# Softmax weights transposed two heads at a time, and value products on quarters of the array

## The chip, the cores and the metric

The kernel runs on one core of one Trainium2 chip. The metric is the device time of one execution in microseconds (us). The engines named here are TensorE (PE: matmuls and transposes, with its weight loads listed apart as PEld), VectorE (DVE), ScalarE (ACT), GpSimd (POOL) and SyncE (SP, which issues every DMA of this kernel).

## The reference

Three stages follow one another: attention over short windows, a gated feed-forward layer and a feed-forward layer with a rational activation. The change lies in the first one.

```python
# attention: q, k, v are [4, 8, 768, 64]; chunks of 32 queries; 8 memory keys per head
for c in range(24):
    keys   = concat(mem_k, k[16 before the chunk : 8 behind it])   # 8 + 16 + 32 + 8 = 64 keys
    scores = q_c @ keys.T / 8
    a = exp(scores - max(scores));  a = a / (sum(a) + 1e-9)
    out[chunk] = a @ values                                        # the same 64 positions of v
x = out, heads side by side                                        # [3072, 512]
x = ((1 / (1 + exp(-(x @ w_gate)))) * (x @ w_val)) @ w_out         # 512 -> 1536 -> 512
h = x @ w_in                                                       # 512 -> 2048
g = (a0 + a1*h + a2*h^2 + a3*h^3) / (1 + |b0|*|h| + |b1|*h^2 + 1e-6)
return g @ w_out2                                                  # 2048 -> 512
```

## The kernel before

**Tiles.** The 3072 tokens are 24 attention tiles `t` of 128 queries: four chunks of 32, all eight heads. Neighbouring chunks go in pairs: a window `g` holds the 104 positions that its two chunks reach together (`WIN` = 104, of which each chunk uses 64, `KEYS`; the second chunk's 64 begin at `OFF1` = 40). The head number is `2r + h`.

**Attention of one tile**, by the names in the code:

- `attn_qk` (line 104): 32 matmuls into two PSUM tiles `sp`, one for each `h`. Each multiplies 32 queries by 64 keys over 64 numbers of a head, so it uses 64 rows and 32 columns of the array. Scores lie with queries on partitions and the 64 keys along the row.
- `attn_max`, `attn_exp`, `attn_sum`: the softmax on VectorE and ScalarE, in the tile `s` (128 x 8 heads x 64 keys).
- `attn_mul` (line 157): two VectorE multiplications, one for each chunk of a pair (64 partitions each), write the weights into a buffer `a` with 104 positions per head. Each chunk's weights go to its own place in the window, and the rest of `a` is zero (set once by GpSimd, lines 67 and 68).
- `attn_t` (lines 170 and 172): eight transposes on TensorE, one per head (128 queries x 104 positions), into two PSUM tiles `tp`, and two ScalarE copies to `at`.
- `attn_pv` (line 184): 16 matmuls into one PSUM tile `xp`, over the 104 positions of a window, 64 columns of the array each, 64 moving columns (the two chunks of the window). Line 192 (ScalarE) and line 193 (VectorE) write it out as a rounded high part and a low part, both in the tile `x`, which four tiles `t` fill together.

In the trace every plain fp32 matmul of lines 104 and 184 has two records, each with a weight load of its own: 64 records for the 32 matmuls of `sp`, 32 for the 16 of `xp`. Transposes have one.

**The feed-forward layers.** All their operands are split into a high and a low part, and three of the four cross products are summed, each a 128x512 matmul. The first layer runs over six blocks `j` of 512 tokens and twelve steps `f`; a step is two groups of 12 matmuls into `h` (line 261) and 12 into `acc` (line 293). The second layer (lines 342 and 381) follows the same way and has no attention in it.

**The order.** It is written out by hand. The attention of tiles 0 to 3 comes first, mixed with the unpacking of the first weights. Then the 72 steps of the first layer run, and a plan gives the attention of the tiles of the next block to certain steps: `attn_qk` and `attn_max` behind the second `h` group, `attn_sum`, `attn_mul`, `attn_pv` and `attn_t` between the two `h` groups. The PSUM tiles `sp`, `tp`, `xp` and `h` share four buffers that are handed out in turn (`psp`). Each engine works through its own list in order.

**The start.** SyncE issues its loads in one queue, in this order: q and k of tiles 0, 1 and 2, v of tiles 1 and 0, q and k of tile 3, three weight pieces of step 0, v of tile 3, the three of step 1, v of tile 2, the three of step 2. Of the v loads, the one for tile 2 is the last that tiles 0 to 3 need.

Of the kernel before, what the change touches and what calls it, by code (L numbers as in the profile page):

```python
# [8 lines left out]
F32 = mybir.dt.float32  # L9
# [4 lines left out]
ACTF = mybir.ActivationFunctionType  # L14
ALU = mybir.AluOpType
# [3 lines left out]
B, H, S, D = 4, 8, 768, 64  # L19
CH, LEFT, RIGHT, NMEM = 32, 16, 8, 8  # L20
NT, DM, DFF1, DFF2 = B * S, H * D, 1536, 2048
P = 128
NF1, NF2 = DFF1 // P, DFF2 // P
KT = DM // P
SB = S // P
NBLK = NT // P
CTX = LEFT + 2 * CH + RIGHT
WIN = NMEM + CTX + NMEM
KEYS = NMEM + LEFT + CH + RIGHT
OFF1 = WIN - KEYS  # L30
NSET = 8
KW, VW = NSET * WIN, 2 * DM
MASKED = -3.0e38
QC = 1.0 + 1e-6
BLOCKS1 = [512] * 6
# [4 lines left out]
def fused_kernel(ctx: ExitStack, tc: tile.TileContext, q, k, v, w1, w2, coef, x2d, w2d, out):  # L40
# [7 lines left out]
    nc = tc.nc  # L48

    const = ctx.enter_context(tc.tile_pool(name="const", bufs=1))  # L50
    wpool = ctx.enter_context(tc.tile_pool(name="w", bufs=32))
    xpool = ctx.enter_context(tc.tile_pool(name="x", bufs=2))
    gpool = ctx.enter_context(tc.tile_pool(name="g", bufs=4))
    tpool = ctx.enter_context(tc.tile_pool(name="t", bufs=11))
    spool = ctx.enter_context(tc.tile_pool(name="s", bufs=4))
    accp = ctx.enter_context(tc.tile_pool(name="acc", bufs=1, space=PSUM))
    psp = ctx.enter_context(tc.tile_pool(name="ps", bufs=4, space=PSUM))
# [1 line left out]
    ident = const.tile([P, P], F32, name="ident")  # L59
    make_identity(nc, ident)  # L60
    cf = const.tile([P, 6], F32, name="cf")
    cab = const.tile([P, 2], F32, name="cab")


    a_buf = [const.tile([P, NSET, WIN], F32, name=f"a{i}") for i in range(2)]
    for a in a_buf:
        nc.gpsimd.memset(a[0:64, :, KEYS:WIN], 0.0)
        nc.gpsimd.memset(a[64:128, :, 0:OFF1], 0.0)

    def t2(name):  # L70
        return tpool.tile([P, 512], F32, tag="t", name=name)

    def ps(name):
        return psp.tile([P, 512], F32, tag="ps", name=name)


    qs, ks, vs, s_sb, sc_ps, at_sb = {}, {}, {}, {}, {}, {}
# [5 lines left out]
        nc.sync.dma_start(out=u, in_=k[t])  # L83

    def load_v(t):
        u = vs[t] = wpool.tile([P, VW], F32, tag="w", name=f"v{t}")
        nc.sync.dma_start(out=u[0:WIN], in_=v[t])

    def edge(t):
        return t % SB in (0, SB - 1)  # L90

    def attn_qk(t):


        qt = qs.pop(t)
        kt = ks.pop(t).rearrange("p (r g w) -> p r g w", r=4, g=2)
        sps = [ps(f"sp{t}_{h}")[:, 0 : 4 * KEYS].rearrange("p (r w) -> p r w", r=4) for h in range(2)]
        for r in range(4):
            for i in range(4):
                c, g = divmod(i, 2)  # L100
                for h in range(2):
                    d = slice(64 * h, 64 * h + 64)
                    o = slice(32 * i, 32 * i + 32)
                    nc.tensor.matmul(  # L104
                        sps[h][o, r],
                        lhsT=qt[d, r, o],
                        rhs=kt[d, r, g, c * OFF1 : c * OFF1 + KEYS],
                        start=True,
                        stop=True,
                    )  # L110
        s = s_sb[t] = tpool.tile([P, NSET, KEYS], F32, tag="t", name=f"s{t}")
        sv = s.rearrange("p (r h) w -> p r h w", h=2)
        if edge(t):
            for h in range(2):
                nc.scalar.activation(out=sv[:, :, h], in_=sps[h], func=ACTF.Copy)
            if t % SB == 0:
                nc.gpsimd.memset(s[0:32, :, NMEM : NMEM + LEFT], MASKED)
            else:
                e = CTX - RIGHT + NMEM - OFF1
                nc.gpsimd.memset(s[96:128, :, e : e + RIGHT], MASKED)  # L120
        else:
            sc_ps[t] = sps
# [22 lines left out]
    rs = {}  # L145
# [6 lines left out]
        nc.vector.reciprocal(out=r, in_=r)  # L152

    def attn_mul(t):
        s, r, a = s_sb.pop(t), rs.pop(t), a_buf[t % 2]
        for lo, c0 in ((0, 0), (64, OFF1)):
            nc.vector.tensor_tensor(
                out=a[lo : lo + 64, :, c0 : c0 + KEYS],
                in0=s[lo : lo + 64],
                in1=r[lo : lo + 64].to_broadcast([64, NSET, KEYS]),  # L160
                op=ALU.mult,
            )

    def attn_t(t):
        a = a_buf[t % 2]
        at_sb[t] = []
        for half in range(2):
            tp = ps(f"tp{t}_{half}")
            for i in range(4):
                nc.tensor.transpose(tp[0:WIN, i * P : (i + 1) * P], a[:, 4 * half + i], ident)  # L170
            at = t2(f"at{t}_{half}")
            nc.scalar.activation(out=at[0:WIN], in_=tp[0:WIN], func=ACTF.Copy)
            at_sb[t].append(at)

    def attn_pv(t, x, n0):
        vt = vs.pop(t)[0:WIN].rearrange("p (g e) -> p g e", g=2)
        ats = at_sb.pop(t)
        xp = ps(f"xp{t}").rearrange("p (r n) -> p r n", r=4)
        for r in range(4):
            at = ats[r // 2][0:WIN].rearrange("p (s c g q) -> p s g c q", s=4, c=2, g=2)  # L180
            for g in range(2):
                for h in range(2):
                    e = (2 * r + h) * D
                    nc.tensor.matmul(  # L184
                        xp[64 * h : 64 * h + 64, r, 64 * g : 64 * g + 64],
                        lhsT=vt[:, g, e : e + D],
                        rhs=at[:, 2 * (r % 2) + h, g],
                        start=True,
                        stop=True,
                    )  # L190
        hi, lo = x[:, :, 0, n0 : n0 + P], x[:, :, 1, n0 : n0 + P]
        nc.scalar.activation(out=hi, in_=xp, func=ACTF.Copy)  # L192
        nc.vector.tensor_tensor(out=lo, in0=xp, in1=hi.bitcast(F32), op=ALU.subtract)

# [203 lines left out]
    def pv(t):  # L400
        j, n0 = t // 4, t % 4 * P
        if n0 == 0:
            xt[j] = xpool.tile([P, KT, 2, 512], F32R, tag="x", name=f"x{j}")
        attn_pv(t, xt[j], n0)
# [54 lines left out]
    for t in range(4, NBLK, 2):  # L459
        j, i = divmod(t, 4)  # L460
        s0 = (j - 1) * NF1 + (5 if i else 0)
        if j == 1:
            s0 = 5 if i else 2
        for o, u in ((0, t), (1, t + 1)):
            at(s0 + o - 2, load_qk, u)
            at(s0 + o, attn_qk, u)
            at(s0 + o, attn_max, u)
            at(s0 + 3, attn_exp, u)
            at(s0 + o + 3, load_v, u)
            at(s0 + o + 3, attn_sum, u)  # L470
            at(s0 + o + 3, attn_mul, u)
            at(s0 + o + 4, attn_t, u)
            at(s0 + o + 5, pv, u)
# [21 lines left out]
    with tc.manual_schedule():  # L495
# [3 lines left out]
        load_qk(1)  # L499
        load_qk(2)  # L500
        load_v(1)
        load_v(0)
        load_qk(3)
        load_w1(0)
# [3 lines left out]
        load_v(2)  # L508
        load_w1(2)
        attn_qk(0)  # L510
        attn_max(0)
        attn_exp(0)
        attn_qk(1)
        attn_qk(2)
        attn_sum(0)
# [5 lines left out]
        conv_scale("1_0_0")  # L521
        attn_exp(2)
        attn_mul(0)
        attn_mul(1)
        attn_max(3)
        attn_t(0)
        attn_sum(2)
        attn_exp(3)
        attn_sum(3)
        attn_t(1)  # L530
        conv_scale("1_0_2")
        attn_mul(2)
# [66 lines left out]
        for si in range(PRE, len(steps2) + LAG2):  # L599
            if si < len(steps2):  # L600
                j, f = steps2[si]
# [19 lines left out]
def _windows(k, mem):  # L621

    import numpy as np

    pad = np.zeros((B, H, LEFT + S + RIGHT, D), k.dtype)
    pad[:, :, LEFT : LEFT + S] = k
    n = S // (2 * CH)
    ctx = np.stack([pad[:, :, 2 * CH * g : 2 * CH * g + CTX] for g in range(n)], axis=2)
    m = np.broadcast_to(mem[:, :, None], (B, H, n, NMEM, D))
    return np.concatenate([m, ctx, m], axis=3)  # L630
# [52 lines left out]
```

## Time and profile before

| | before |
|---|---|
| time, median of 3 runs | 1221.54 us (1219.17 to 1221.76) |
| profiled execution | 1218.23 us, of which the span of the trace is 1216.5 us |
| TensorE busy | 1193.0 us, 98% of the span |
| VectorE busy | 906.7 us, 75% |
| ScalarE busy | 760.5 us, 63% |
| DMA traffic | 99.25 MB, mean 82 GB/s |

The share of busy time is a mean over the whole span; what matters for the change is the stretch in which attention runs, and which wait ends last there. Matmul records overlap (the next begins before the last one ends), so the cost of a small matmul is not its record's length but the distance to the next one: the length of a run of them, less one record, divided by the number less one.

### The profile page before, as it was taken

How to read it: one execution, taken by the hardware profiler on the slowest of the kernel's cores; microseconds unless marked ns; L12 is line 12 of the kernel's file. 1: busy time of each engine (PE TensorE's matmuls, PEld its weight loads, DVE VectorE, ACT ScalarE, POOL GpSimd, SP SyncE). 2: the span in 40 equal slices, each digit the busy share in tenths (PEclk: the TensorE clock that was granted, in tenths of full speed). 3: DMA queues.
4: the chain of work that ended last, by engine and by line, in shares of the span. 5: the costliest groups of instructions: out<-in, count | busy, mean ns of one | idle time of the engine just before them, and what ended most of it. 6: DMA issues, size and time to landing. Idle time of an engine off the chain costs nothing.

```text
span 1216.5 us, 18667 instructions
## 1 busy us (share of the span) xinstructions
PE 1193.0 (98%) x7392; PEld 981.5 (81%) x7392; DVE 906.7 (75%) x1458; ACT 760.5 (63%) x1302; POOL 3.5 (0%) x19
## 2 busy tenths in 40 slices
PE   4999999999999999999999999999999999999998
PEld 4787788888888888888888888888888888888887
DVE  6899566657566664765566589998898898898885
ACT  4987354545454554545555588777676776766765
POOL 0000000000000000000000000000000000000000
PEclk9899999999999999999999999999999999999999
DMA  9863041424243332512342110010100100100000
GB/s 309 313 197 123 23 143 53 134 88 136 66 146 108 107 103 75 169 54 80 126 152 87 33 63 18 10 53 9 44 18 9 53 18 1 52 18 1 35 1 35
DMA packets 39327, 99.25 MB, mean 82 GB/s; under 512 B 4488, under 2 KB 4488, under 8 KB 39240
## 3 DMA queue, kind: packets, MB, share of 16 engines
q1 hardware_dynamic: 39240, 98.06, 25.3%
q8 instruction: 58, 0.95, 0.3%
q14 instruction: 29, 0.24, 0.1%
HBM read 77.07 MB, written 20.97 MB: 81 GB/s over the span
## 4 chain that ended last, share of the span: by engine, by line
PE 89%; DVE 5%; ACT 3%; DMA 2%; issue 1%; SPq 0%; POOL 0%; DVEq 0%; POOLq 0%; ACTq 0%
PE h L261 28%; PE acc L381 21%; PE h L342 21%; PE acc L293 14%; PE xp L184 2%; PE tp L170 1%; DVE wf L218 1%; DVE wp L248 1%; DVE wf L225 1%; PE sp L104 1%; DMA v<-v_in 1%; DMA st<-w_in 1%; ACT g L279 1%; DVE sg L273 0%; ACT wp L244 0%
## 5 line engine op out<-in xcount | busy, mean ns | idle before, releaser
L261 PE MATMUL h<-x,wp 128*128 128x512 f32 x1728 | 414.8, 393 | 2.6 <-ACT x L192 1.6
L261 PEld LDWEIGHTS h<-x,wp 128*128 128x128 f32 x1728 | 323.8, 189 | 70.8 <-ACT x L192 1.8
L342 PE MATMUL h<-x,wp 128*128 128x512 f32 x1152 | 276.6, 389 | 0.0
L381 PE MATMUL acc<-wp,g 128*128 128x512 f32 x1152 | 276.0, 389 | 0.0
L381 PEld LDWEIGHTS acc<-wp,g 128*128 128x128 f32 x1152 | 216.3, 188 | 44.9
L342 PEld LDWEIGHTS h<-x,wp 128*128 128x128 f32 x1152 | 216.3, 188 | 44.8
L293 PE MATMUL acc<-g,wp 128*128 128x512 f32 x864 | 211.0, 393 | 0.0
L293 PEld LDWEIGHTS acc<-g,wp 128*128 128x128 f32 x864 | 160.7, 188 | 35.2
L279 ACT ACTIVATE g<-sg 128x512 fp32r<-128x512 f32 x72 | 45.5, 632 | 183.5 <-DVE sg L273 183.4
L350 ACT ACTIVATE t<-h,cf 128x512 f32<-128x512 f32 x96 | 74.7, 778 | 127.0 <-PE h L342 126.0
L273 DVE TENSOR_TENSOR sg<-sg,h 128x512 f32<-128x512 f32 x72 | 49.5, 687 | 123.8 <-PE h L261 106.4
L248 DVE TENSOR_TENSOR wp<-wf,wp 128x512 fp32r<-128x512 f32 x216 | 136.3, 685 | 0.1
L244 ACT ACTIVATE wp<-wf 128x512 fp32r<-128x512 f32 x216 | 120.8, 620 | 5.9 <-DVE c L225 4.0
L353 DVE TENSOR_TENSOR t<-t,h 128x512 f32<-128x512 f32 x96 | 65.9, 686 | 45.0 <-ACT hh L352 43.2
L270 ACT ACTIVATE sg<-h 128x512 f32<-128x512 f32 x72 | 42.9, 596 | 86.1 <-PE h L261 86.0
L280 DVE TENSOR_TENSOR g<-sg,g 128x512 fp32r<-128x512 f32 x72 | 49.9, 693 | 51.2 <-ACT g L279 51.2
L354 DVE SCALAR_TENSOR_TENSOR t<-t,cf,h 128x512 f32<-128x512 f32 x96 | 71.8, 748 | 3.4
L368 DVE SCALAR_TENSOR_TENSOR qq<-qq,y 128x512 f32<-128x512 f32 x96 | 65.9, 686 | 11.2 <-ACT y L363 11.2
L362 ACT ACTIVATE y<-qq,qc 128x512 f32<-128x512 f32 x96 | 70.0, 729 | 5.3 <-DVE qq L355 4.6
L355 DVE SCALAR_TENSOR_TENSOR qq<-hh,cab,qq 128x512 f32<-128x512 f32 x96 | 71.7, 747 | 0.0
L369 DVE SCALAR_TENSOR_TENSOR t<-t,cf,y 128x512 f32<-128x512 f32 x96 | 71.7, 747 | 0.0
L370 DVE SCALAR_TENSOR_TENSOR t<-qq,t 128x512 f32<-128x512 f32 x96 | 66.5, 693 | 3.3
(53 smaller groups left out, 930.8 us busy)
## 6 DMA issues: line engine op xcount, KB each, us to landing
st<-w_in SPq DMA_DIRECT2D x68, 512.0 KB, 7.1
k<-k_in SPq DMA_DIRECT2D x24, 416.0 KB, 6.9
v<-v_in SPq DMA_DIRECT2D x24, 416.0 KB
w2d<-c SPq DMA_DIRECT2D x32, 256.0 KB, 2.0
w2f<-w2d SPq DMA_DIRECT2D x32, 256.0 KB, 3.2
q<-q_in SPq DMA_DIRECT2D x24, 256.0 KB, 11.4
x2d<-x2s SPq DMA_DIRECT2D x24, 256.0 KB, 2.8
x2f<-x2d SPq DMA_DIRECT2D x24, 256.0 KB
```

What stands on the lines that cost most here:

```text
L244: nc.scalar.activation(out=wp[key][:, 0], in_=src, func=ACTF.Copy)
L248: nc.vector.tensor_tensor(out=t[:, 1], in0=src, in1=t[:, 0].bitcast(F32), op=ALU.subtract)
L261: nc.tensor.matmul(pt, lhsT=w[:, a, kt * P : (kt + 1) * P], rhs=x[:, kt, b, c0 : c0 + n], start=(kt == 0 and i == 0), stop=(kt == KT - 1 a ...
L293: nc.tensor.matmul(acc[j][d][:, c0 : c0 + n], lhsT=w[:, a, d * P : (d + 1) * P], rhs=g[:, b, 0:n], start=(f == 0 and c0 == 0 and i == 0), ...
L342: nc.tensor.matmul(hp, lhsT=w[:, a, kt * P : (kt + 1) * P], rhs=x[:, kt, b], start=(kt == 0 and i == 0), stop=(kt == KT - 1 and i == 2),)
L350: nc.scalar.activation(out=t, in_=hp, func=ACTF.Identity, scale=cf[:, 3:4], bias=cf[:, 2:3])
L354: nc.vector.scalar_tensor_tensor(out=t, in0=t, scalar=cf[:, 1:2], in1=hp, op0=ALU.add, op1=ALU.mult)
L355: nc.vector.scalar_tensor_tensor(out=qq, in0=hh, scalar=cab[:, 1:2], in1=qq, op0=ALU.mult, op1=ALU.add)
L362: nc.scalar.activation(out=y, in_=qq, func=ACTF.Abs_reciprocal_sqrt, bias=qc[:, 0:1])
L369: nc.vector.scalar_tensor_tensor(out=t, in0=t, scalar=cf[:, 0:1], in1=y, op0=ALU.add, op1=ALU.mult)
L370: nc.vector.scalar_tensor_tensor(out=t, in0=qq, scalar=2.0, in1=t, op0=ALU.subtract, op1=ALU.mult)
L381: nc.tensor.matmul(acc[j][m], lhsT=g[:, a, m * P : (m + 1) * P], rhs=w[:, b], start=(f == 0 and i == 0), stop=(f == NF2 - 1 and i == 2),)
```

## The change

The weights are no longer spread over a window of 104 positions. `attn_mul` multiplies in place, in one instruction over all 128 partitions, so that `s` holds 64 keys per head, and two heads lie side by side in 128 numbers. `attn_t` transposes such a pair at once: four transposes of 128x128 into one PSUM tile, and one copy. Behind it the 64 keys of head `h` = 0 lie on partitions 0 to 63 and those of `h` = 1 on partitions 64 to 127. `attn_pv` multiplies each chunk and each head by itself: 32 matmuls of 64 keys by 64 columns of the array by 32 queries, on one quarter of the array each (rows by `h`, columns by `e`, the low bit of the pair number), into two PSUM tiles, one for each `h`, that are written out in two halves. The values come laid out by chunk, 64 keys each on 128 partitions (512 KB per tile instead of 416 KB), and the rows of the first layer's weights are put into the new order of heads on the host. The GpSimd memsets of `a` go, and the pool `t` has 12 buffers instead of 11.

```diff
     def load_v(t):
-        u = vs[t] = wpool.tile([P, VW], F32, tag="w", name=f"v{t}")
-        nc.sync.dma_start(out=u[0:WIN], in_=v[t])
+        u = vs[t] = wpool.tile([P, 4, 4, D], F32, tag="w", name=f"v{t}")
+        nc.sync.dma_start(out=u, in_=v[t])
...
     def attn_mul(t):
-        s, r, a = s_sb.pop(t), rs.pop(t), a_buf[t % 2]
-        for lo, c0 in ((0, 0), (64, OFF1)):
-            nc.vector.tensor_tensor(
-                out=a[lo : lo + 64, :, c0 : c0 + KEYS],
-                in0=s[lo : lo + 64],
-                in1=r[lo : lo + 64].to_broadcast([64, NSET, KEYS]),
-                op=ALU.mult,
-            )
+        s, r = s_sb[t], rs.pop(t)
+        nc.vector.tensor_tensor(out=s, in0=s, in1=r.to_broadcast([P, NSET, KEYS]), op=ALU.mult)
 
     def attn_t(t):
-        a = a_buf[t % 2]
-        at_sb[t] = []
-        for half in range(2):
-            tp = ps(f"tp{t}_{half}")
+        s = s_sb.pop(t).rearrange("p (r h) w -> p r (h w)", h=2)
+        tp = ps(f"tp{t}")
+        for r in range(4):
+            nc.tensor.transpose(tp[:, r * P : (r + 1) * P], s[:, r], ident)
+        at = at_sb[t] = t2(f"at{t}")
+        nc.scalar.activation(out=at, in_=tp, func=ACTF.Copy)
...
+        vt, at = vs.pop(t), at_sb.pop(t).rearrange("p (r q) -> p r q", r=4)
+        xps = [ps(f"xp{t}_{h}")[:, 0:256].rearrange("p (k n) -> p k n", k=2) for h in range(2)]
+        for k in range(2):
             for i in range(4):
-                nc.tensor.transpose(tp[0:WIN, i * P : (i + 1) * P], a[:, 4 * half + i], ident)
-            at = t2(f"at{t}_{half}")
-            nc.scalar.activation(out=at[0:WIN], in_=tp[0:WIN], func=ACTF.Copy)
-            at_sb[t].append(at)
...
+                o = slice(32 * i, 32 * i + 32)
+                for e in range(2):
+                    for h in range(2):
+                        d = slice(64 * h, 64 * h + 64)
+                        nc.tensor.matmul(
+                            xps[h][64 * e : 64 * e + 64, k, o],
+                            lhsT=vt[d, i, 2 * k + e],
+                            rhs=at[d, 2 * k + e, o],
+                            start=True,
+                            stop=True,
+                        )
+        for h in range(2):
+            hi, lo = (x[:, 2 * h : 2 * h + 2, b, n0 : n0 + P] for b in range(2))
+            nc.scalar.activation(out=hi, in_=xps[h], func=ACTF.Copy)
+            nc.vector.tensor_tensor(out=lo, in0=xps[h], in1=hi.bitcast(F32), op=ALU.subtract)
```

The first place is TensorE in step 7 of block 0, between the two `h` groups, where the products of one tile and the transposes of the next stand (x8 means eight instructions alike). Before:

```order
L261 MATMUL h_7_0_0_1236<-x_368,wp_0_7_0_1090 128x512 x12
L184 MATMUL xp_1255<-at_0_1127,v_965 64x64 x8
L184 MATMUL xp_1255<-at_1_1134,v_965 64x64 x8
L170 MATMUL tp_0_1274<-ident,a_91 104x128 x4
L170 MATMUL tp_1_1281<-ident,a_91 104x128 x4
L261 MATMUL h_7_1_0_1288<-x_368,wp_0_7_1_1092 128x512 x12
```

The same place now, its beginning (the two `xp` rows alternate until there are 32 of them) and its end:

```order
L250 MATMUL h_7_0_0_1265<-x_344,wp_0_7_0_1127 128x512 x12
L172 MATMUL xp_0_1284<-at_1164,v_1003 64x32
L172 MATMUL xp_1_1285<-at_1164,v_1003 64x32
L172 MATMUL xp_0_1284<-at_1164,v_1003 64x32
L172 MATMUL xp_1_1285<-at_1164,v_1003 64x32
```

```order
L172 MATMUL xp_1_1285<-at_1164,v_1003 64x32
L157 MATMUL tp_1322<-ident,s_901 128x128 x4
L250 MATMUL h_7_1_0_1329<-x_344,wp_0_7_1_1129 128x512 x12
```

No instruction of another kind is moved past these: 16 products become 32 and eight transposes become four, at the same place in the step.

The second place is ScalarE in the start, from the copies of `xp` for tiles 1 and 2 to that for tile 3, with the unpacking of weights (`st`, `wp`) between them. Before:

```order
L192 ACTIVATE x_368<-xp_426 128x4x128
L192 ACTIVATE x_368<-xp_445 128x4x128
L213 ACTIVATE st_1_2_133<-st_1_2_133 128x512
L214 ACTIVATE st_1_2_133<-st_1_2_133 128x512
L244 ACTIVATE wp_0_0_1_466<-wf_366 128x512
L244 ACTIVATE wp_0_0_2_470<-wf_422 128x512
L192 ACTIVATE x_368<-xp_474 128x4x128
```

Now:

```order
L181 ACTIVATE x_344<-xp_0_445 128x2x128
L181 ACTIVATE x_344<-xp_1_446 128x2x128
L202 ACTIVATE st_1_2_127<-st_1_2_127 128x512
L203 ACTIVATE st_1_2_127<-st_1_2_127 128x512
L233 ACTIVATE wp_0_0_1_485<-wf_342 128x512
L233 ACTIVATE wp_0_0_2_489<-wf_403 128x512
L181 ACTIVATE x_344<-xp_0_493 128x2x128
L181 ACTIVATE x_344<-xp_1_494 128x2x128
```

Each copy has become two of half the size, and the four weight instructions between them stand where they stood.

## Rows read from the trace of the kernel before

**Rows 1.** Two stretches: length, busy us (instructions) of PE, PEld, DVE, ACT, POOL, clock, DMA share, GB/s.
```profile
0.00:34.08 34.08, 16.05 (x418) 13.52 (x418) 23.40 (x48) 18.65 (x35) 2.38 (x12) 0.92 0.97 320
34.08:590.00 555.92, 554.26 (x4229) 452.50 (x4230) 364.28 (x621) 314.87 (x546) 1.17 (x7) 1.00 0.37 116
```
**Rows 2.** Waits of TensorE: us in total, times, longest.
```profile
PE sp L104 <- DMA k<-k_in: 11.8, 4, 5.0
PE xp L184 <- DMA v<-v_in: 2.2, 1, 2.2
PE tp L170 <- DVE s L137: 1.0, 1, 1.0
```
**Rows 3.** Timeline of PE in block 1: start, length (both us), group, count.
```profile
183.71 1.03 PE L170 MATMUL tp<-ident,a 128*104 128x128 f32 x8
...
190.09 2.88 PE L261 MATMUL h<-x,wp 128*128 128x512 f32 x12
192.90 1.15 PE L184 MATMUL xp<-at,v 104*64 104x64 f32 x32
193.99 1.08 PE L170 MATMUL tp<-ident,a 128*104 128x128 f32 x8
...
197.76 0.86 PE L104 MATMUL sp<-k,q 64*32 64x64 f32 x64
```
**Rows 4.** Records of tp, xp, sp behind 40 us: ns min/median/max.
```profile
L170 PE MATMUL tp<-ident,a x160: 272/273/317, 88.3 to 574.6; 128*104 128x128 f32 x160
L184 PE MATMUL xp<-at,v x640: 221/222/270, 98.5 to 584.0; 104*64 104x64 f32 x160
L104 PE MATMUL sp<-k,q x1280: 212/216/243, 55.3 to 541.5; 64*32 64x64 f32 x183
L104 PEld LDWEIGHTS sp<-k,q x1280: 102/106/108, 55.3 to 541.4; 64*32 64x32 f32 x183
```
**Rows 5.** Timeline: sp begins; the first h behind xp; an h within a run.
```profile
92.02 0.12 PEld L104 LDWEIGHTS sp<-k,q 64*32 64x32 f32 x4 [0.35 <-ACT st L214]
...
110.94 0.50 PE L261 MATMUL h<-x,wp 128*128 128x512 f32 x1
...
211.94 0.39 PE L261 MATMUL h<-x,wp 128*128 128x512 f32 x1
```
**Rows 6.** Groups by line and form: busy us, mean ns | idle before.
```profile
L157 DVE TENSOR_TENSOR a<-s,r 64x512 f32<-64x512 f32 x48 | 32.8, 684 | 1.1
L172 ACT ACTIVATE at<-tp 104x512 f32<-104x512 f32 x48 | 26.0, 596 | 0.0
L193 DVE TENSOR_TENSOR x<-xp,x 128x512 fp32r<-128x512 f32 x24 | 16.6, 691 | 33.9 <-ACT x L192 33.9
L192 ACT ACTIVATE x<-xp 128x512 fp32r<-128x512 f32 x24 | 14.3, 595 | 10.5 <-PE xp L184 10.5
L137 DVE TENSOR_TENSOR s<-sp,m 128x256 f32<-128x256 f32 x32 | 12.0, 416 | 0.0
L115 ACT ACTIVATE s<-sp 128x256 f32<-128x256 f32 x16 | 5.1, 372 | 4.2 <-PE sp L104 4.2
```
**Rows 7.** Chain of waits in the start: start, length, what.
```profile
16.49 11.38 DMA v<-v_in
...
28.01 1.67 PE xp L184 x32
29.70 0.60 ACT x L192
```
**Rows 8.** Timeline of PE from 34 us.
```profile
34.08 5.15 PE L261 MATMUL h<-x,wp 128*128 128x512 f32 x12 [0.30 <-DVE x L193]
```
**Rows 9.** Two stretches of the start, columns as in Rows 1.
```profile
2.50:16.50 14.00, 4.69 (x256) 3.95 (x256) 8.36 (x20) 1.92 (x5) 0.59 (x3) 1.00 1.02 327
...
28.43:38.67 10.24, 8.32 (x69) 6.67 (x66) 8.33 (x15) 8.97 (x17) 0.00 (x0) 0.50 1.03 401
```
**Rows 10.** DMA issues: size and count of the v loads.
```profile
v<-v_in SPq DMA_DIRECT2D x24, 416.0 KB
```

More of the change, by code (lines that the diff above doesn't have):

```diff
@@ L31 @@
 NSET = 8
-KW, VW = NSET * WIN, 2 * DM
+KW = NSET * WIN
 MASKED = -3.0e38
@@ L53, in fused_kernel @@
     gpool = ctx.enter_context(tc.tile_pool(name="g", bufs=4))
-    tpool = ctx.enter_context(tc.tile_pool(name="t", bufs=11))
+    tpool = ctx.enter_context(tc.tile_pool(name="t", bufs=12))
     spool = ctx.enter_context(tc.tile_pool(name="s", bufs=4))
@@ L62, in fused_kernel @@
     cab = const.tile([P, 2], F32, name="cab")
[L65 to L68, printed above, removed]
     def t2(name):
@@ L99, in attn_qk @@
             for i in range(4):
-                c, g = divmod(i, 2)
+                g, c = divmod(i, 2)
                 for h in range(2):
@@ L175, in attn_pv @@
[L175 to L193, printed above, removed]
+        s, r = s_sb[t], rs.pop(t)
@@ new lines, in attn_mul, with attn_pv @@
+        nc.vector.tensor_tensor(out=s, in0=s, in1=r.to_broadcast([P, NSET, KEYS]), op=ALU.mult)
+    def attn_t(t):
+        s = s_sb.pop(t).rearrange("p (r h) w -> p r (h w)", h=2)
[4 more added lines that the diff above has]
+        nc.scalar.activation(out=at, in_=tp, func=ACTF.Copy)
+    def attn_pv(t, x, n0):
+        vt, at = vs.pop(t), at_sb.pop(t).rearrange("p (r q) -> p r q", r=4)
+        xps = [ps(f"xp{t}_{h}")[:, 0:256].rearrange("p (k n) -> p k n", k=2) for h in range(2)]
+        for k in range(2):
+            for i in range(4):
+                o = slice(32 * i, 32 * i + 32)
[13 more added lines that the diff above has]
+            nc.vector.tensor_tensor(out=lo, in0=xps[h], in1=hi.bitcast(F32), op=ALU.subtract)
@@ L639, with by_head @@
     a = {n: np.asarray(x) for n, x in inputs.items()}
-    qd = a["q"].reshape(B, 4, 2, SB, 2, 2, CH, D).transpose(0, 3, 2, 7, 1, 5, 4, 6)
+    qd = a["q"].reshape(B, 4, 2, SB, P, D).transpose(0, 3, 2, 5, 1, 4)
     kd = _windows(a["k"], a["mem_k"]).reshape(B, 4, 2, SB, 2, WIN, D)
     kd = kd.transpose(0, 3, 2, 6, 1, 4, 5)
-    vd = _windows(a["v"], a["mem_v"]).reshape(B, H, SB, 2, WIN, D)
-    vd = vd.transpose(0, 2, 4, 3, 1, 5)
+    vw = _windows(a["v"], a["mem_v"]).reshape(B, 4, 2, SB, 2, WIN, D)
+    vd = np.stack([vw[..., 0:KEYS, :], vw[..., OFF1:WIN, :]], axis=5)
+    vd = vd.transpose(0, 3, 2, 6, 4, 5, 1, 7)
+    heads = [2 * (2 * (kt % 2) + e) + kt // 2 for kt in range(KT) for e in range(2)]
     def cols(w, nf):
         return w.reshape(KT, P, nf, P).transpose(1, 2, 0, 3).reshape(P, nf, 512)
+    def by_head(w):
+        return w.reshape(H, D, -1)[heads].reshape(DM, -1)
     def rows(w, nf):
@@ L653 @@
     w1 = np.stack(
-        [cols(a["moe_w_gate"], NF1), cols(a["moe_w_val"], NF1), rows(a["moe_w_out"], NF1)], axis=2
+        [cols(by_head(a["moe_w_gate"]), NF1), cols(by_head(a["moe_w_val"]), NF1), rows(a["moe_w_out"], NF1)],
+        axis=2,
     )
@@ L660 @@
         "k_in": kd.reshape(NBLK, P, KW),
-        "v_in": vd.reshape(NBLK, WIN, VW),
+        "v_in": vd.reshape(NBLK, P, 4, 4, D),
         "w1_in": w1.reshape(P, NF1, 3 * 512),
```

## The prediction, written before the changed kernel ran

> **What bounds the kernel now.** I began with the busy times of the engines: TensorE's fills nearly the whole span, VectorE's three quarters. A mean says little, so next came the same numbers by stretch [rows 1]: until 34.08 us TensorE is busy for 16.05 us, less than half; from there to 590 us, where the rest of the attention lies, for 554.26 of 555.92 us. VectorE is at 364.28 in that stretch, ScalarE at 314.87, DMA at 0.37 of its time. TensorE's waits [rows 2] say the same: the long ones are for loads of k and v, all in the start, and the one for the softmax is 1.0 us, once. So there are two problems: a start that loads set, with four of the 24 tiles, and then a TensorE that never rests, with the other twenty. In the second, what counts is how long TensorE takes over a tile; work taken from other engines gives nothing there.
>
> What a tile costs there I read from the timeline of a block [rows 3] and the length of single records [rows 4]. Eight transposes are (1.03 - 0.27) / 7 = 0.109 us apart, in another run (1.08 - 0.27) / 7 = 0.116. Thirty-two records of `xp` are (1.15 - 0.22) / 31 = 30.0 ns apart; from their start to that of the next group it is 193.99 - 192.90 = 1.09 us. Sixty-four records of `sp` are (0.86 - 0.22) / 63 = 10.2 ns apart.
>
> **Transposes: eight become four.** Four go, at 0.109 us each (the more frequent of the two distances): 0.43 us per tile. Each of the rest still moves 128 columns; only its weights grow from 104 columns to 128. What a load of weights takes shows where nothing hides it: the first `h` behind `xp` has a record of 0.50 us, where one within a run has 0.39 [rows 5]: 0.11 us for 128 columns, which just fits beside a transpose of 0.109. Bounds: 0.46 with the other distance; 0.35 if the load of the 24 columns more (0.02 us at that rate) shows in each of the four; nothing at all if load and transpose stop overlapping, a rival below.
>
> **Products: 16 become 32, on quarters.** Records go from 32 to 64 per tile. Before, a matmul uses half of the array's columns, so two can be under way: 30.0 ns apart is 60 ns in each half. After, four can be under way. The rows give three prices for 64 records:
> - as `sp`, which also has 64 rows to a record and has eight places in the array: 64 x 10.2 = 0.65 us, 0.31 less than the 32 x 30.0 = 0.96 us before;
> - by place: a record in one quarter must load 64 columns of weights as before. A load of 64 columns alone costs 0.05 us (the longest `xp` record, the first of a run, is 270 ns where the median is 222; `sp`, 32 columns, 243 for 216, half of it [rows 4]). That is near the 60 ns in which each half now takes a record. The 32 moving columns instead of 64 then save nothing, because the load sets the pace: 60 ns / 4 = 15 ns apart, 64 x 15.0 = 0.96 us, no change;
> - as before whatever the size: 64 x 30.0 = 1.92 us, 0.96 more.
>
> I take the middle one. It needs weights to be loaded in four quarters at once, and the start of an `sp` run shows that: four loads, of two row halves and two column places, lie within 0.12 us [rows 5], where one alone is at least 0.102 [rows 4]. The end near the first price is possible, if the 60 ns come from the moving columns instead.
>
> **Other engines, in the middle stretch.** Per tile VectorE loses 2 x 0.684 for the multiplication and gains one of 128x512, as long as the 0.691 of line 193; two halves of 0.416 (the nearest row of that size) replace that one: 0.54 us less. ScalarE loses one copy of 0.596 and gets two of 0.372 for 0.595: 0.45 less [rows 6]. TensorE hides both; cost nothing, gain nothing. If they were not hidden, they would be gains of some 10 us in all. The two `xp` tiles and one `tp` take three PSUM buffers where one and two were taken, so the next `h` and `sp` get buffers freed as long ago as now; between an `xp` and the next `sp` there is an `h` group of 2.88 us [rows 3], in which the two halves (2 x 0.372 + 0.416 = 1.2 us) are read out. Twenty loads of v that are larger move 2 MB more in 556 us, under DMAs that are busy for 0.37 of it. The one wait for the softmax, 1.0 us, may shrink, since the multiplication ends 0.68 us earlier; I leave it in the range.
>
> **The start.** Here the end is set by loads: the chain shows v of tile 2 landing at 27.87, its products, their copy, ScalarE's work on weights and the copy of tile 3 [rows 7], and at 34.08 the `h` run [rows 8]. Four v loads stand in the queue up to there, 416 KB each [rows 10], now 512: 393 kB (decimal) more, at 327 GB/s [rows 9] 1.20 us. What stands on ScalarE behind them moves along; the copy of tile 2 takes 2 x 0.372 - 0.595 = 0.15 more, while `h` can begin when the first half of tile 3 is out (0.416 for 0.691: 0.28 less). The `h` run starts 1.2 + 0.15 - 0.28 = 1.1 us later. Against that: from 28.43 to 38.67 the granted clock is 0.50, that is 1.2 GHz [rows 9], and twelve `h` take 5.15 us there [rows 8] instead of 2.88 [rows 3]. `h` now spends 4.6 us in it; starting 1.1 later it spends 3.5, and gets back half of 1.1. Net +0.6 us. If the slow stretch falls elsewhere, all 10.2 us of it may lie on `h`, which costs 10.2 / 2 - 4.6 / 2 = 2.8 more; ends of -0.5 and +3.4. The memsets on GpSimd end before anything waits for them: nothing.
>
> **Sum.** Against the profiled execution, 1218.23 us: 20 x 0.43 = 8.6 less, products 0, start +0.6: 1210.2. The median shown is 3.3 us above that execution, so for it 1213.5 us.
>
> **Rivals.**
> 1. *The products get faster too.* Priced as `sp`: 20 x 0.31 = 6.2 less, 1207.3. For it: the same 64 rows, smaller moving operand. Against: twice the weight columns of `sp`. 0.15.
> 2. *A small matmul costs the same whatever its size* (slower). If 30.0 ns is a floor for one record, 32 records more cost 0.96 us per tile; it decides as soon as this is above the 0.43 from the transposes, that is at over 21.7 ns per record: 20 x (0.96 - 0.43) + 0.6 = +11.2, 1232.7. The same number comes out if two row halves cannot work at once beside two column halves. Against it stands `sp` at 10.2 ns. For it, that no row shows 64 columns on 64 rows. 0.13. The Trainium skill has a rule of this kind: TensorEngine Tiling, section Performance Considerations, puts some 60 cycles of overhead on every matmul and advises against tiling a dimension that is already small, and TensorE: Matmul & The Clock Gate (section "Wait — 56ns, not 53.3ns?") gives about 25 ns from start to start as the least. By that, an estimate, 64 records would take 1.6 us and the change would lose some 4 us. The trace disagrees with it at 10.2 ns for `sp`.
> 3. *The transposes gain nothing*: 128 columns of weights no longer hide beside 128 moving ones, each takes twice as long, and the four cost what the eight did. 1221.54 + 0.6 = 1222.1. Against: 0.11 us of load fits. 0.05.
> 4. *The start goes badly*: the slow stretch lies wholly on `h`: 1213.5 + 2.8 = 1216.3. 0.05.
>
> **How the numbers follow.** The forecast has 0.62; its own range, from the start's ends and 0.35 to 0.46 us per tile from the transposes, is 1211 to 1218, and a bit lower if the wait goes. Nothing under 0.2% (2.4 us) can be told from no change here: faster means below 1219.1, slower above 1224.0. The forecast and rivals 1 and 4 are faster, 0.82, less a little for their upper tails: 0.80. Rival 3 and these tails are the same: 0.07. Rival 2 is slower: 0.13. The range leaves rival 2 out and reaches from rival 1 with a good start (1204) to rival 3 (1222).
>
> **What would show it.** In the timeline of a step: `tp` x4 with the next group 0.4 us behind its start instead of 0.83; `xp` x64 in about 1.15 us, the same as x32 now, and so 15 ns apart. At 1.9 us or more, rival 2 holds; at 0.85, rival 1. VectorE and ScalarE lower by some 10 us each, with no gain from it. First `h` run at 35 us. I am wrong if the `xp` group is not as long as before, if TensorE begins to wait between 35 and 580 us, or if the start moves by more than 3 us.

## The result, and the profile after

| | before | after |
|---|---|---|
| time, median | 1221.65 us (1219.17 to 1222.94, 4 runs) | 1208.01 us (1207.91 to 1208.78, 4 runs) |
| profiled execution (span) | 1218.23 us (1216.5) | 1208.78 us (1207.0) |

The ratio of the two is 0.9893, with an interval of 0.9878 to 0.9909: 13.6 us faster, where 8.0 were forecast, and below the forecast's own range of 1211 to 1218. Transposes and products did what was written; the start did the opposite, and nothing else was off by as much.

**The middle stretch.** The same two stretches as in [rows 1], of the changed kernel (line numbers are lower by 6 to 13 from here on: `tp` is line 157, `xp` 172, `sp` 98, `h` 250, `acc` 282):

```profile
0.00:34.00 34.00, 18.80 (x535) 15.66 (x536) 22.46 (x51) 18.87 (x38) 0.94 (x8) 0.81 0.96 370
34.00:575.00 541.00, 538.68 (x4760) 438.13 (x4759) 346.91 (x613) 301.97 (x538) 1.18 (x7) 1.00 0.35 119
```

TensorE is nearly as full as it was (idle for 2.3 us instead of 1.7), and the stretch is shorter. What a tile costs there stands in the timeline of the block of [rows 3]:

```profile
181.26 0.60 PE L157 MATMUL tp<-ident,s 128*128 128x128 f32 x4
...
187.19 2.88 PE L250 MATMUL h<-x,wp 128*128 128x512 f32 x12
190.00 1.14 PE L172 MATMUL xp<-at,v 64*64 64x32 f32 x64
191.06 0.66 PE L157 MATMUL tp<-ident,s 128*128 128x128 f32 x4
191.48 3.01 PE L250 MATMUL h<-x,wp 128*128 128x512 f32 x12
```

Four transposes take 0.60 us where eight took 1.03; (0.60 - 0.27) / 3 = 0.11 us apart, as before. Sixty-four records of `xp` take 1.14 us where 32 took 1.15, and the next group begins 191.06 - 190.00 = 1.06 us after them, where it was 1.09. The length of single records (ns, min/median/max, 40 to 590 us) is needed to turn that into a distance, as with [rows 4]:

```profile
L157 PE MATMUL tp<-ident,s x80: 270/272/329, 86.1 to 565.2; 128*128 128x128 f32 x80
L172 PE MATMUL xp<-at,v x1280: 211/219/241, 95.9 to 574.5; 64*64 64x32 f32 x183
```

(1.14 - 0.22) / 63 = 14.6 ns apart, twice as dense as the 30.0 of before. A block of twelve steps holds four tiles, so the distance between the same `tp` in two blocks gives the price of four tiles with no reading of single records. In block 2 the changed kernel, and the kernel before, have:

```profile
290.37 0.60 PE L157 MATMUL tp<-ident,s 128*128 128x128 f32 x4
```
```profile
294.57 1.03 PE L170 MATMUL tp<-ident,a 128*104 128x128 f32 x8
```

290.37 - 181.26 = 109.11 us now, 294.57 - 183.71 [rows 3] = 110.86 before: 1.75 us per block, 0.44 per tile. VectorE and ScalarE became lighter, much as worked out, by groups (busy us, mean ns), against [rows 6]:

```profile
L182 DVE TENSOR_TENSOR x<-xp,x 128x256 fp32r<-128x256 f32 x48 | 18.1, 419 | 31.6 <-ACT x L181 31.4
L150 DVE TENSOR_TENSOR s<-s,r 128x512 f32<-128x512 f32 x24 | 16.3, 687 | 0.7
L181 ACT ACTIVATE x<-xp 128x256 fp32r<-128x256 f32 x48 | 15.8, 382 | 12.4 <-PE xp L172 12.4
L159 ACT ACTIVATE at<-tp 128x512 f32<-128x512 f32 x24 | 14.2, 596 | 0.0
```

One wait in this stretch grew. In block 0 TensorE, before and now, comes to a PSUM buffer whose scores `sp` VectorE has not yet read:

```profile
100.67 1.05 PE L170 MATMUL tp<-ident,a 128*104 128x128 f32 x8 [1.01 <-DVE s L137]
```
```profile
97.75 1.13 PE L172 MATMUL xp<-at,v 64*64 64x32 f32 x62 [1.53 <-DVE s L131]
```

Before, it was the first `tp` that came to it, behind all the products. Now it is the second `xp` tile, two records into them, so the products no longer fill part of that time: 1.53 us for 1.01.

**The start.** The chain of waits of the changed kernel, where [rows 7] had v of tile 2 at 27.87 us:

```profile
15.54 9.11 DMA v<-v_in
24.65 0.14 issue
24.79 2.20 PE xp L172 x73
26.99 1.65 issue
28.64 1.78 PE xp L172 x55
30.42 0.64 ACT x L181 x2
```

The load lands at 24.65 us, 3.2 earlier, though more is moved ahead of it. The long `h` run, at 34.08 in [rows 8], begins at 30.84:

```profile
30.84 7.52 PE L250 MATMUL h<-x,wp 128*128 128x512 f32 x24 [0.48 <-ACT x L181]
```

The rate of the loads shows why. The same stretch, 9.00 to 16.50 us (length, busy time of PE, PEld, DVE, ACT, POOL, clock, DMA share, GB/s), first of the kernel before, then of the changed one:

```profile
9.00:16.50 7.50, 2.35 (x128) 2.03 (x128) 6.99 (x18) 0.92 (x3) 0.00 (x0) 1.00 1.04 309
```
```profile
9.00:16.50 7.50, 3.30 (x133) 2.95 (x134) 6.53 (x19) 1.58 (x3) 0.00 (x0) 1.00 1.03 408
```

The DMA engines are fully busy in both, and moved 309 GB/s before and 408 now. In the DMA records the packets of 4 KB of the first 28 us, those of v and of the weights together, last 208 ns in the mean before (1375 of them) and 163 now (1792). In the kernel before, those that begin between 28 and 32 us, when no v is in the queue, last 163 ns too.

TensorE's waits, as in [rows 2], have new names. In the start there are the softmax's multiplication (line 150) and 1.65 us for nothing that the profile shows (the "issue" in the chain); the wait for line 131 is the one in block 0:

```profile
PE sp L98 <- DMA k<-k_in: 6.8, 3, 4.6
PE sp L98 <- DVE s L150: 4.1, 1, 4.1
PE xp L172 <- issue: 1.6, 1, 1.6
PE xp L172 <- DVE s L131: 1.5, 1, 1.5
```

**The clock, and what the two profiled executions add up to.** The stretch at 1.2 GHz (granted clock 0.50) that [rows 9] has from 28.43 to 38.67 us lies elsewhere now, and there is a second one in block 0:

```profile
21.00:34.65 13.65, 10.73 (x205) 8.97 (x204) 10.99 (x23) 10.87 (x25) 0.00 (x0) 0.50 1.03 405
...
99.50:102.92 3.42, 3.42 (x9) 2.65 (x8) 3.42 (x7) 3.42 (x8) 0.00 (x0) 0.50 0.45 108
```

The first came after waits of TensorE of 4.1 and 1.1 us, the second after the 1.53 us above. The long `h` run spends 34.65 - 30.84 = 3.8 us in the first. The second lies on twelve `h` behind a `tp`, which take 4.59 us where such a group takes 3.01 in the block shown above:

```profile
99.22 4.59 PE L250 MATMUL h<-x,wp 128*128 128x512 f32 x12
```

From the `tp` of block 1 to the end the changed kernel needs 7.0 us less, four blocks at 1.75. Up to that `tp` it is only 183.71 - 181.26 = 2.45 us ahead, although `h` begins 3.2 us earlier and block 0 holds four tiles too: 1.6 us go to the second slow stretch, and 1.0 to the way from the beginning of the long `h` run to the first `acc`, 13.92 us for 12.94, 0.8 of it a wait for weights. Whether the other three timed executions had the second stretch no trace shows; their mean granted clock is 0.999 or 1.000, and 0.992 here. So the two profiled executions are only 9.5 us apart where the medians are 13.6: the one before lay 3.4 us under its median, this one 0.8 over.

### The profile page after: what moved, and what is told of

It is laid out like the page before. It is cut to its first block, busy times and chain, and to the rows that moved or that the text cites. A ratio compares the mean times of both kernels' runs of the same rounds, so it can differ in the third digit from the quotient of the medians.

```text
span 1207.0 us, 19977 instructions
## 1 busy us (share of the span) xinstructions
PE 1185.7 (98%) x8064; PEld 973.7 (81%) x8064; DVE 891.4 (74%) x1458; ACT 749.2 (62%) x1302; POOL 2.1 (0%) x15
## 3 DMA queue, kind: packets, MB, share of 16 engines
q8 instruction: 63, 1.03, 0.4%
## 4 chain that ended last, share of the span: by engine, by line
PE 92%; DVE 3%; ACT 2%; DMA 2%; issue 0%; SPq 0%; POOL 0%; POOLq 0%; DVEq 0%
PE h L250 29%; PE acc L370 22%; PE h L331 22%; PE acc L282 15%; PE xp L172 2%; PE sp L98 1%; PE tp L157 1%; DMA st<-w_in 1%; DMA v<-v_in 1%; DVE wf L207 1%; DVE wp L237 1%; DVE wf L214 1%; ACT st L202 0%; ACT st L203 0%; ACT g L268 0%
```

## The experiments

My theory after the result: the middle stretch gave what was forecast, 0.43 us per tile by the transposes alone, and the rest came from the start, because a load that fills 104 partitions is slow for its bytes. Rivals: the faster loads were chance; the relief of VectorE and ScalarE did it; the products got faster after all. Every experiment was timed beside the kernel before, whose medians in the three sets were 1222.87, 1221.78 and 1222.24 us. None repeats the changed kernel, so its 1208.01 is from the first set of runs, in which the kernel before had 1221.65: counted against the kernel before of their own set, the losses below would be up to 1.2 us smaller.

**The load alone, on 128 partitions.** In the kernel before:

```diff
-        nc.sync.dma_start(out=u[0:WIN], in_=v[t])
+        nc.sync.dma_start(out=u[0:128], in_=v[t])
-        "v_in": vd.reshape(NBLK, WIN, VW),
+        "v_in": np.pad(vd.reshape(NBLK, WIN, VW), ((0, 0), (0, 128 - WIN), (0, 0))),
```

> The kernel before, with nothing changed but the v loads: the values are padded with zeros on the host and each load fills 128 partitions (512 KB) instead of 104 (416 KB). Theory A (a load of 104 partitions is slow for its bytes, and that is what set the start): v of tile 2 lands about 3 us earlier than the 27.87 us of before although more is moved, the long run of h begins at about 31 us, and the whole is 2 to 4 us faster than before, about 1218.5 us. Theory B (the loads of the changed kernel were faster by chance, or because of something else in it): v lands later by the 1.2 us of the added bytes, and the whole is the same or 1 us slower.

1216.01 us against 1222.87 for the kernel before: 6.9 us faster (ratio 0.9945, 0.9928 to 0.9962), with nothing changed but 96 KB of zeros in each load. Theory A, and by more than it said. Its timeline and its stretch from 9 us:

```profile
32.22 9.98 PE L261 MATMUL h<-x,wp 128*128 128x512 f32 x33 [0.54 <-DVE x L193]
```
```profile
9.00:16.50 7.50, 2.33 (x131) 2.04 (x128) 7.24 (x18) 0.63 (x1) 0.00 (x0) 1.00 1.03 410
```

410 GB/s as in the changed kernel, 4 KB packets of 163 ns, v of tile 2 at 25.53 us. The chain of waits up to this `h` run no longer holds a load of v; it goes through VectorE, with the old multiplication in it:

```profile
22.24 0.68 DVE a L157
...
22.94 0.69 DVE a L157
```

**112 partitions.** The same edit with 112.

> As the run with 128 partitions, with 112 (448 KB), a multiple of 16 that is not a power of two. Theory A1 (what is slow is a number of rows that the 16 DMA engines cannot share out evenly): as fast as 128 or 0.3 us faster still. Theory A2 (what is slow is any load that does not fill the partitions in the way that 128 do): packets as long as with 104, no gain. Theory B: 0.6 us slower than before.

1219.92 us (ratio 0.9978, 0.9969 to 0.9987): 3 us faster, less than half of the gain. In its trace:

```profile
9.00:16.50 7.50, 1.63 (x93) 1.36 (x93) 7.02 (x18) 0.77 (x2) 0.00 (x0) 1.00 1.03 318
```

318 GB/s, packets of 214 ns: the packets are as long as with 104. A1, that a multiple of 16 is enough, falls. The trace also has the semaphore updates by which DMAs report that they have landed: 4432 in all with loads of 112 as with loads of 128, and 4384 with 104, two fewer for each of the 24 loads. So a load of 112 lands in as many parts as one of 128, and the packets are long all the same. That the run was still 3 us faster fits neither theory; v of tile 2 lands at 29.83 us, and its `h` run begins later than in [rows 8]:

```profile
35.53 6.70 PE L261 MATMUL h<-x,wp 128*128 128x512 f32 x22 [0.60 <-DVE x L193]
```

**The changed kernel with its loads cut.** In two parts of 104 and 24 partitions, and, in a later set, of 64 and 64:

```diff
-        nc.sync.dma_start(out=u, in_=v[t])
+        for p in (slice(0, 104), slice(104, P)):        # the other run: (0, 64), (64, P)
+            nc.sync.dma_start(out=u[p], in_=v[t, p])
```

> The changed kernel with each v load in two: partitions 0 to 103 and 104 to 127, the same bytes. Theory A: the slow packets come back, v of tile 2 lands 3 us later than the 24.65 us of the changed kernel, and the whole is 2 to 4 us slower, about 1211 us. Theory B: the start stays as it is, but for some 0.4 us for each further issue, 1208 to 1209 us.

> The changed kernel with each v load in two halves of 64 partitions. If what makes the packets long is any load of fewer than 128 partitions: packets over 200 ns and 3 us or more lost, 1211 us or above. If it is a number of partitions that does not divide evenly (104, 112, 24): packets of 163 ns as with 128, and at most 1 us lost to the further issues.

1215.48 us (ratio to before 0.9941, 0.9926 to 0.9956) and 1214.85 us: 7.5 and 6.8 us of the 13.6 are lost, about twice what was expected of the first. The stretch from 9 us, of the first and of the second:

```profile
9.00:16.50 7.50, 1.17 (x64) 0.96 (x64) 5.82 (x16) 0.63 (x1) 0.00 (x0) 1.00 1.03 245
```
```profile
9.00:16.50 7.50, 1.17 (x64) 0.96 (x64) 5.89 (x16) 0.63 (x1) 0.00 (x0) 1.00 1.03 277
```

The rate is 245 and 277 GB/s and the packets last 229 and 231 ns. With 64 the number divides evenly, and the packets are long all the same: every kernel here whose loads of v filled fewer than the 128 partitions had them, none with loads of 128 did. In the first of the two the `h` run begins at 40.53 us:

```profile
40.53 2.04 PE L251 MATMUL h<-x,wp 128*128 128x512 f32 x3 [1.48 <-ACT x L182]
```

Cutting a load also gives eight issues instead of four up to tile 3, so not all of this is the packets.

**Eight transposes again.** In the changed kernel each is issued twice, to the same place:

```diff
-        for r in range(4):
+        for r in (0, 1, 2, 3, 0, 1, 2, 3):
             nc.tensor.transpose(tp[:, r * P : (r + 1) * P], s[:, r], ident)
```

> The changed kernel with each of its four transposes per tile issued twice, to the same place. If a transpose costs TensorE 0.109 us wherever it stands and nothing else comes of it: 20 x 0.435 = 8.7 us slower in the middle stretch, 1216.7 us, and 1.74 us in each block of four tiles. If the gain was in the wait for VectorE or in the copies instead: under 3 us slower.

1215.97 us: 8.0 us more than the changed kernel, for 8.7 expected. The same `tp` in blocks 1 and 2:

```profile
181.45 1.03 PE L157 MATMUL tp<-ident,s 128*128 128x128 f32 x8
...
292.32 1.03 PE L157 MATMUL tp<-ident,s 128*128 128x128 f32 x8
```

110.87 us per block, that of the kernel before to a hundredth, with everything else of the change in place. In the middle stretch the transposes are the whole gain.

**Products by row half.** All products of one head of a pair, then all of the other, so that two places are left to work at once:

```diff
-        for k in range(2):
-            for i in range(4):
-                o = slice(32 * i, 32 * i + 32)
-                for e in range(2):
-                    for h in range(2):
+        for h in range(2):
+            for k in range(2):
+                for i in range(4):
+                    o = slice(32 * i, 32 * i + 32)
+                    for e in range(2):
```

> The changed kernel with its 32 products in another order: all of head h = 0 first (rows 0 to 63 of the array), then all of h = 1, so that at any time only the two column halves of one row half can work. If four quarters work at once in the changed kernel and each place takes a record in 60 ns: 30 ns apart here, the xp group 1.9 us long instead of 1.14, some 0.9 us per tile and 18 us in all slower, 1226 us. If only two places ever work at once, or if a record has a floor of its own of 15 to 17 ns: no change.

1222.19 us: 14.2 us more than the changed kernel, all that the change had brought. The group in the same block:

```profile
191.45 1.85 PE L172 MATMUL xp<-at,v 64*64 64x32 f32 x64
193.24 0.66 PE L157 MATMUL tp<-ident,s 128*128 128x128 f32 x4
```

1.85 us for the 64 records, (1.85 - 0.22) / 63 = 25.9 ns apart, for the 30 expected. So the quarters do work at once, and there is no floor of 15 ns in the number 14.6: half the places, nearly twice the distance. Each place takes a record in 4 x 14.6 = 58 ns with four at work and 2 x 25.9 = 52 with two.

**Twice the moving columns.** Each product moves 64 queries instead of 32, written one over another:

```diff
-                o = slice(32 * i, 32 * i + 32)
+                o = slice(32 * min(i, 2), 32 * min(i, 2) + 64)
```

> The changed kernel with each product moving 64 columns instead of 32 (the queries of two chunks, written one over the other, so that the attention output is not the reference's); the number of products, their weights and their order stay. If the load of 64 weight columns sets the pace: xp groups as long as before (1.14 us), at most 0.1 us per tile more, 1208 to 1210 us. If the moving columns set it: up to twice as long, 0.9 us per tile, up to 1226 us.

1207.54 us, no different from 1208.01. In its block:

```profile
188.71 1.16 PE L172 MATMUL xp<-at,v 64*64 64x64 f32 x64
189.80 0.65 PE L157 MATMUL tp<-ident,s 128*128 128x128 f32 x4
```

1.16 us for 1.14. Thirty-two moving columns cost what 64 do, and the load of 64 weight columns (0.05 us alone [rows 4]) is what is left as the pace of a place. This run does not take that load away, so it shows that the moving columns are not the pace, and not directly that the load is.

**The work of VectorE and ScalarE put back.**

```diff
-        nc.vector.tensor_tensor(out=s, in0=s, in1=r.to_broadcast([P, NSET, KEYS]), op=ALU.mult)
+        for p in (slice(0, 64), slice(64, P)):
+            nc.vector.tensor_tensor(out=s[p], in0=s[p], in1=r[p].to_broadcast([64, NSET, KEYS]), op=ALU.mult)
-        nc.scalar.activation(out=at, in_=tp, func=ACTF.Copy)
+        for _ in range(2):
+            nc.scalar.activation(out=at, in_=tp, func=ACTF.Copy)
```

> The changed kernel with the work that it took from VectorE and ScalarE put back: the multiplication in two halves of 64 partitions, and the copy of the transposed weights done twice. If TensorE hides both engines, as the prediction has it: no change outside the start, within 1.5 us of 1208 us. If the relief of VectorE and ScalarE was part of the gain: 4 to 14 us slower.

1211.74 us: 3.7 us more, between the two expectations. The middle stretch:

```profile
34.00:575.00 541.00, 537.62 (x4694) 438.02 (x4694) 360.95 (x633) 315.22 (x561) 1.17 (x7) 1.00 0.34 118
```

VectorE and ScalarE are back at the load of [rows 1], and TensorE is busy for 537.62 us of 541.00 where it was for 538.68. There they are hidden but for 1.1 us, all of it in block 0, where the wait for line 131 grows from 1.53 to 2.18 us and one of 0.43 joins it. The long `h` run begins at 33.45 us instead of 30.84:

```profile
33.45 7.97 PE L252 MATMUL h<-x,wp 128*128 128x512 f32 x26 [0.40 <-ACT x L183]
```

By the traces 2.6 us stand in the start, where four tiles go through VectorE and ScalarE with little of TensorE's to hide them, and 1.1 in block 0; together that is what the medians differ by. With the fast loads these engines have come onto the path in the start. They were not far from it: [rows 2] leaves out this wait of the kernel before, at 22.28 and 23.70 us:

```profile
PE tp L170 <- DVE a L157: 2.1, 2, 1.8
```

**The load of v for tile 2 earlier.** First only `load_v(2)` ahead of `load_w1(1)`; then, besides, `conv_scale("1_1_2")` from ahead of `pv(3)` to behind it:

```diff
+        load_v(2)
         load_w1(1)
-        load_v(2)
...
         pv(2)
-        conv_scale("1_1_2")        # the second run only
...
         pv(3)
+        conv_scale("1_1_2")
```

> The changed kernel with the load of v for tile 2 issued ahead of the three weight pieces of step 1 instead of behind them. If the start is still set by that landing (24.65 us): v lands some 3.9 us earlier (1.57 MB at 405 GB/s), the weight pieces 1.3 us later, and the long h run begins 1.5 to 2.5 us earlier: 1205.5 to 1206.5 us. If the chain through VectorE and ScalarE has become as long as the loads: under 1 us faster, since the work on the later weight pieces stands on ScalarE ahead of the copy of tile 3.

> As the run with v of tile 2 loaded early, and two ScalarE instructions on a weight piece of step 1 moved from ahead of the products of tile 3 to behind them. If ScalarE's order holds tile 3 back there: a further 1.1 us earlier, 1204.5 to 1205.5 us. If VectorE does, or if step 1 then waits for its weights: no further gain, or 1 us lost.

1208.57 and 1208.67 us: no gain in either. The load did land 3 us earlier, at 21.61 us in the first, but the chain there now reads:

```profile
22.60 3.84 PE xp L172 x135
26.44 2.31 issue
28.76 1.77 PE xp L172 x49
```

The gap of "issue" has grown from 1.65 to 2.31 us and ends at 28.76 us where it ended at 28.64. In both timelines it stands at the same record, 55 before the last of tile 3, whenever v came. A packet of 16 KB on the queue that the page calls "instruction" runs from 26.2 to 27.3 us in the changed kernel and from 26.3 to 27.4 here. Six traces have the gap (the changed kernel, eight transposes, twice the columns, more work, and the two here), and in all six it ends 1.3 to 1.5 us behind the end of that packet, wherever the packet lies (from 25.5 us with eight transposes to 28.8 with more work). That points to TensorE's own instructions, of which the products of a tile now take twice as many, arriving late. The products by row half have such a packet too, from 26.5 to 27.6 us, and no gap; TensorE is slower there and comes to the same record at some 29 us, an estimate from 192 records in 8.77 us. No run takes the packet away, so the cause of the gap stays argued. In the second run step 1 then waited 2.0 us for its weights.

**The kernel before once more.**

> The kernel before once more, for a second trace of its start: its timed runs lie 1 to 6 us above the execution that was profiled. If the load of v is what varies, v of tile 2 lands later than 27.87 us here and the long h run begins later than 34.08; if only the clock varies, both are the same and more of the first h steps lie at 1.2 GHz. The packets of the v loads are long (over 200 ns) in any case.

1221.31 us, and in its second trace the `h` run begins at 36.31 us instead of 34.08:

```profile
36.31 5.93 PE L261 MATMUL h<-x,wp 128*128 128x512 f32 x19 [0.28 <-DVE x L193]
```

Packets last 222 ns, and v of tile 2 lands at 29.78 us instead of 27.87; the stretch at 1.2 GHz is as long as before, 28.96 to 39.20 us. So the start moved, by 2.2 us between two traces of one kernel, and 1.9 of them are the landing of v. The execution behind the rows ahead of the prediction was one of the quick ones.

The four traces of this kernel, with loads of 104 (twice), 112 and 128 partitions, share something simple. Time less the beginning of the long `h` run is 1218.23 - 34.08 = 1184.15, 1220.40 - 36.31 = 1184.09, 1219.62 - 35.53 = 1184.09 and 1216.36 - 32.22 = 1184.14 us. What the load does to the time, it does ahead of that run. By this, an estimate, a median execution of the kernel before, 1222.87 us, begins it at 38.8, and one with loads of 128, 1216.01, at 31.9.

## Why the prediction was right or wrong

**Transposes: right.** 0.43 us per tile forecast, 1.75 us per block of four measured. Twenty tiles make 8.75 us; the run that issues them twice again lost 8.0.

**Products: right, and both conditions of the reason held.** 15.0 ns apart forecast, 14.6 measured; the price went from 1.09 to 1.06 us per tile. The two conditions behind it were tried one by one: four quarters at work (with two, 25.9 ns), and moving columns that cost nothing beside the weight load (with twice as many, 1.16 us for 1.14). That the weight load is the pace was not shown by itself.

**Rival 1 has nearly the measured time and is wrong.** It gave 1207.3, by products priced like `sp`. Had I looked at the total alone, I would have taken it for shown. The timeline names the place: the products did not become cheaper by more than 0.03 us per tile.

**Rivals 2 and 3: wrong.** The rule of a least time per matmul would have shown itself at over 21.7 ns per record; the trace has 14.6. Transposes are 0.11 us apart with 128 weight columns as with 104.

**Rival 4, and the clock.** The slow stretch of the start did not lie wholly on `h`. It began 7.4 us earlier than before, and `h` spent 3.8 us in it where 3.5 were forecast; that is near, but by luck, since I had `h` move and the stretch stay. The second one, in block 0, is in no term of the sum; it lay wholly on `h` and cost the profiled execution 1.6 us.

**VectorE and ScalarE: hidden in the middle stretch but for 1.1 us, and not in the start.** In the start I let the chain run through the load and priced only the copies of tiles 2 and 3. With their work put back the kernel loses 3.7 us. In the middle stretch I looked at the PSUM buffers of the next `h` and `sp` alone; the wait that I thought might shrink grew, because the second `xp` tile now meets it.

**The start: the failed step.** "393 kB (decimal) more, at 327 GB/s [rows 9] 1.20 us", and from that +0.6 us net. Measured, the load lands 3.2 us earlier and the `h` run begins 3.2 us earlier in the profiled execution; and the one edit that belongs to the load is worth 6.9 us in the kernel before. A start that moves by more than 3 us was one of the prediction's own signs of being wrong, and so was a TensorE that waits behind 35 us (0.8 us for weights at 39.60, 1.53 in block 0). The step failed in taking 327 GB/s as the rate of the DMA engines. It was a mean over two kinds of loads. The other line of [rows 9] said so: 401 GB/s behind 28.43 us, when no v is in the queue, with the DMA engines as busy as at 327. I used that line for its clock alone. A stretch in which v runs has 309 GB/s, and 408 where the same stretch has none of 104 partitions. Adding bytes made the load a full one, and it got faster.

The Trainium skill speaks of this, and I did not weigh it. DMA: Bandwidth & Descriptors (section "Why a DMA increments its semaphore by 16 and not by 1") has a load run on the largest number of engines, up to 16, that divides its partitions: by that 13 for 104, 16 for 112 and 64. SBUF — State Buffer (section "Door 1: The DMA port swizzle") has the bandwidth follow the memory ports that the partitions reach, all 16 for 0 to 127 and eight for 0 to 63. The runs agree that 128 is the fast number. That an even share over the engines is enough they do not bear out: 112 lands in as many parts as 128, by the semaphore updates, and has packets of 214 ns. So the number of engines does not account for 112. What makes the packets long there and with 104 is open; only 64 follows from the ports.

**The sum.** The transposes by their run (8.0) and the load by its run (6.9) make 14.9 us, which from 1222.87 leads to 1208.0, and 1208.01 was measured. That it fits to the hundredth is luck: from 1221.65, the kernel before in the changed kernel's own set, it leads to 1206.8. The relief of VectorE and ScalarE, 3.7 us, I take for no third term beside them: 2.6 of it lie in the start, and there the chain of waits goes through these engines only once the load is fast. No run gives the relief to the kernel before with its slow loads, so this is argued. A version that beats the changed kernel was not found.

**What stays open.** That the 6.9 us of the load all lie ahead of the `h` run follows from the four traces above. In the profiled executions `h` begins only 34.08 - 32.22 = 1.9 us earlier because that of the kernel before was a quick one; against its second trace it is 36.31 - 32.22 = 4.1 us, and no trace of a median execution was taken. Why the run with 112 partitions gained 3 us is open. Its trace is 0.8 us shorter than the second one of the kernel before, although v of tile 2 lands at the same time in both (29.83 and 29.78 us); with 112 the 64 records of `xp` behind the landing take 2.08 us at full clock, with 104 they take 3.68 at 1.2 GHz.

## What to carry to other kernels

Where TensorE is never idle, price a change by how many instructions of what pace it issues there, and check the price by the distance between the same instruction in two rounds of the loop: it holds to hundredths where sums of busy time do not. Tiles of the array pay only in an order that keeps neighbours in the list on different places; with the wrong loop outermost the same 32 products cost everything the change had gained. Before costing a load by its bytes, read the rate in a stretch where that kind of load runs: here padding to 128 partitions moved 23% more bytes for these loads and was worth 6.9 us.

## What was not expected of the hardware

- With loads of v of 104, 112, 64 or 104 and 24 partitions the packets of 4 KB of the first 28 us lasted 208 to 231 ns in the mean, with loads of 128 partitions 163 ns, with the DMA engines fully busy in both.
- A product on a quarter of the array costs the same with 32 and with 64 moving columns (64 records in 1.14 and 1.16 us).
- TensorE stood still for 1.65 us (2.31 in another run) in the middle of the products of one tile, at the same record in both, with nothing in the profile that it waited for. In six traces the gap ended 1.3 to 1.5 us behind the end of a 16 KB packet of the queue "instruction".
